# Attention with a top-32 mask: GpSimd's three instructions of a step in another order, and the token step moved up in VectorE's step

## The chip, the cores and the metric

One core of a Trainium2 chip runs the whole program in one launch. The metric is device microseconds (us) of one execution; the figure for a kernel is the median of its runs. Engines are named as in the profile: PE (TensorE), DVE (VectorE), ACT (ScalarE), POOL (GpSimd), SP (the DMA queue).

## What is computed

Three layers follow each other: masked attention, a mixture of experts that sends each token to one expert, and a mixing layer with a Fourier transform and a feed-forward net. The change touches the first alone.

```python
scores = scale * np.matmul(q, k.transpose(0, 1, 3, 2))          # 4 x 8 heads, 576 x 576, head_dim 64
kth = np.partition(scores, -32, axis=-1)[..., -32:-31]          # 32nd largest of each row
scores = np.where(scores >= kth, scores, -1000000000.0)
scores = scores - np.max(scores, axis=-1, keepdims=True)
attn = np.exp(scores)
attn = attn / (np.sum(attn, axis=-1, keepdims=True) + 1e-09)
return np.matmul(attn, v)
```

The gate of the experts is computed from the attention output, token by token, with a carry along the sequence (a token can keep the expert of the token before it).

## The kernel before, in words

**Tiles and steps.** The 4 x 8 heads make 16 pairs, each pair nine tiles of 128 query rows by 576 keys: 144 tiles. The loop over n does, in every step, one operation of each kind for a tile that is some steps behind (table `OFF`). A step of one tile has on each engine:

- PE: the score products `s` (L408), the transposes `tp`/`tr`/`trq` with the mask added (L514, L515), the product with v `u` (L533).
- ACT: the copy of the scores `ss` (L423), `g` (L450: the sign of score against a candidate, with a count beside it), `bb` (L492: the mask), `et` (L521, L522: exponentials), `st_x` (L540, L542: results).
- DVE: eight `MAX8` on pieces of the row (L429, "segments"), five operations on the 64 candidates (L439 to L443), then, for a tile three steps older, `MAX8` over the masked row `y` (L460) and the choice of the threshold `sc` (L466, `select`).
- POOL: `kb` (L471, `lift`: threshold times a constant, one column), and two long passes over 576 columns, `y = ss * g` (L455, `below`) and `z = ss - max` (L501, `shifted`). At a pair's last tile two small copies `ext` (L504) follow `z`.

**Who needs whom.** `sc` needs L460, which needs `y` of the same tile, made two steps earlier. `kb` needs `sc` of the same step; `bb` needs `kb` a step later. `y` needs `g`, made a step earlier. `z` is read by the transposes four steps later. `ss` has six buffers, `z` five, `y` two.

**Order.** Every engine runs its own instructions in the order in which the program issues them. Two strings set it: `ORDER` (L748) is the order of the kinds within a step, where `m` is `z`, `y` is `y` and `dve` the whole of VectorE's part; `DVE_ORDER` (L749) is the order inside that part, which takes the next item of a queue per letter: `s` a segment, `c` a candidate operation, `y` in turn L460, `sc` and `kb` (this one goes to POOL), `t` a token step.

**Token steps.** When a batch of 36 tiles is through (n = 43, 79, 115), the generator `tokens` (L547 on) is queued; each `t` advances it to its next `yield`. Its steps are small DVE operations on tokens and experts (L553 to L644), two POOL products `xtok` in each of its first five steps (L558), PE transposes into the PSUM tiles `tr` and `u`, and five POOL scatters `xs_d` (L656, with a memset L662) at its end. Three batches run their token steps inside the loop; in the third, `ranks` (L223 to L244) follows. The fourth batch runs after the loop.

`tr` is a part of the PSUM tile `trk` that the token steps use too, and every DVE operation that touches it waits for ACT's last use of that tile: `et` (L522) of every second tile, `hi`, `vt` and `in_v` (L323, L368, L379) in the others.

Of the kernel before, what the change touches and what calls it, by code (L numbers as in the profile page):

```python
# [20 lines left out]
B, H, S, D = 4, 8, 576, 64  # L21
# [84 lines left out]
def body(ctx: ExitStack, tc, q, k, v, w_gate, w_local, w1, w2, ch1, ch2, ts, tcd, tnd, tid, out, dbg=None):  # L106
# [149 lines left out]
    def attention(exact):  # L256
# [3 lines left out]
        with ExitStack() as ph:  # L260
# [456 lines left out]
            if exact:  # L717
                for o in zops:
                    o()
                for n in range(n_tile):  # L720
                    i, t = divmod(n, 9)
# [23 lines left out]
            tok, prep, wops = [], [], []  # L745
            OFF = dict(u=8, s=-1, S=-1, t=6, av=7, b=5, m=2, e=6, c=1, y=2, z=4)
            WARM = 64
            ORDER = "t u s m p b e dve y S c av"  # L748
            DVE_ORDER = "ycyscsscsyctscscss"  # L749

            def step_dve(n):
                segs = seg_ops(n) if ok(n) else []
# [9 lines left out]
                queues = dict(c=cnds, s=segs, y=ys, t=[tokstep])  # L762
                for o in DVE_ORDER:
                    if queues[o]:
# [11 lines left out]
            def prep_step(eng):  # L776
                if prep and prep[1] == eng:
                    prep[1] = next(prep[0], "")

            OPS = dict(u=step_u, s=scores, S=evac_s, t=trans, av=av, b=step_b, m=shifted, e=evac_e,  # L780
                       c=count, y=below)
            for n in range(n_tile + 1 + max(OFF.values())):
                i, t = divmod(n, 9)
# [3 lines left out]
                if (n - OFF["t"]) % 2:  # L787
                    prep_step("pe")
                for o in ORDER.split():
                    if o == "dve":  # L790
# [24 lines left out]
            if "kth" in dbg:  # L815
                ACT.dma_start(dbg["kth"], kth)

    attention(False)
    def rows_of(ix, n, em):

# [93 lines left out]
    with tc.If(slow > 0):  # L914
        failed = nc.values_load(fail_i[0:1, 0:1], min_val=0, max_val=1)
        with tc.If(failed > 0):
            attention(True)
        overflow()
# [557 lines left out]
```

## Time and profile before

| | us |
|---|---|
| median of three runs | 1330.04 |
| lowest, highest | 1327.12, 1330.62 |
| profiled execution | 1326.02 |
| span of the profiled execution | 1324.2 |
| attention, loop and drain | about 9 to 557 |
| busy DVE, ACT, POOL over the span | 917.2, 695.9, 535.2 |

The span runs from the first to the last instruction. Busy times of the whole span mix three layers; the change concerns the first 560 us, where the stretches without token steps (9 to 133, 252 to 278, 383 to 410 us: "plain" below) have to be told from those with them. The profile's wait lists name the engine that ended an idle time; where two instructions of different engines overlap and one is longer than usual, no idle time shows, only the longer duration.

### The profile page before, as it was taken

To read this page: it belongs to the slowest core of one execution; us is meant where nothing else is said; L and a number is where in the kernel's file an instruction comes from. 1 tells how busy PE (TensorE), PEld (TensorE's weight loads), DVE (VectorE), ACT (ScalarE), POOL (GpSimd) and SP (SyncE) were. 2 spreads that over 40 slices of the span, in tenths; PEclk is the share of its full clock that TensorE was granted. 3 is DMA by queue.
4 is the path that set the end of the run, shared out by engine and by line. 5 is a ranking of instruction groups with operands and counts; after the bars stand their busy time and mean duration, and the time that the engine had idled before them with its cause. 6 is when DMAs were issued, how large, how long until landed. Compare 5 with 4: busy or idle time off the path is not lost. (4 is left out here: it accounts for less than half of the span.)

```text
span 1324.2 us, 25516 instructions
## 1 busy us (share of the span) xinstructions
PE 1209.5 (91%) x8601; PEld 1090.9 (82%) x8601; DVE 917.2 (69%) x3567; ACT 695.9 (53%) x1752; POOL 535.2 (40%) x693
## 2 busy tenths in 40 slices
PE   6999899898889888299999997888999999999997
PEld 4999788887778777188888886778999999999996
DVE  7999899999999997456566665775763444443222
ACT  6999888898889886144444453232321222221110
POOL 5888777888698877311100011451210000000111
PEclk9999989899999999599999999689999999999999
DMA  4656524343344212386666674654230100100111
GB/s 111 191 141 191 128 68 99 89 109 82 90 102 96 68 28 102 107 292 226 221 210 218 221 238 144 202 159 125 73 128 1 64 32 33 63 2 1 49 48 49
DMA packets 127208, 152.25 MB, mean 115 GB/s; under 512 B 68192, under 2 KB 72536, under 8 KB 126955
## 3 DMA queue, kind: packets, MB, share of 16 engines
q1 hardware_dynamic: 121994, 133.34, 34.7%
q0 software_dynamic: 5072, 17.19, 3.6%
q8 instruction: 69, 1.13, 0.4%
q14 instruction: 73, 0.59, 0.1%
HBM read 92.05 MB, written 32.79 MB: 94 GB/s over the span
## 5 line engine op out<-in xcount | busy, mean ns | idle before, releaser
L429 DVE MAX8 cd<-ss 128x8 f32<-128x72 f32 x1152 | 216.2, 218 | 1.6 <-ACT ss L423 1.4
L1391 DVE SCALAR_TENSOR_TENSOR fhl<-f,fhh 128x256 fp32r<-128x256 f32 x144 | 61.0, 424 | 207.3 <-ACT fhh L1390 207.1
L533 PE MATMUL u<-in_v,et 128*128 128x74 f32 (+1 forms) x1600 | 188.9, 268 | 14.9 <-ACT st_x L540 9.6
L1390 ACT ACTIVATE fhh<-f 128x256 fp32r<-128x256 f32 x144 | 55.1, 383 | 279.2 <-PE f L1386 279.2
L533 PEld LDWEIGHTS u<-in_v,et 128*128 128x128 f32 (+1 forms) x1600 | 179.4, 183 | 24.7 <-ACT st_x L540 16.2
L455 POOL TENSOR_TENSOR y<-ss,g 128x576 f32<-128x576 f32 x144 | 184.9, 1284 | 24.1 <-ACT st_x L540 10.3
L501 POOL TENSOR_TENSOR z<-ss,mt 128x576 f32<-128x576 f32 x144 | 167.1, 1160 | 11.8 <-DVE cd L429 9.6
L1411 POOL DMA_INDIRECT out_dram<-ut,orow x18 | 17.4, 969 | 319.7 <-DVE ut L1407 317.7
L450 ACT ACTIVATE g<-ss,mt 128x576 bf16<-128x576 f32 x144 | 120.0, 834 | 28.9 <-DVE mt L443 26.9
L514 PE MATMUL tp<-ident,z 128*128 128x128 f32 x576 | 120.4, 289 | 15.0 <-DVE lo L326 13.9
L408 PE MATMUL s<-kt,qp 128*128 128x288 f32 x640 | 127.9, 329 | 2.8 <-DVE qp L357 1.6
L492 ACT ACTIVATE bb<-ss,kb 128x576 bf16<-128x576 f32 x144 | 117.9, 819 | 8.7 <-POOL kb L471 8.7
L423 ACT ACTIVATE ss<-s 128x288 f32<-128x288 f32 x288 | 112.5, 472 | 4.4 <-PE s L408 2.7
L460 DVE MAX8 y<-y 128x8 f32<-128x576 f32 x144 | 106.8, 742 | 10.8 <-POOL y L455 10.7
L515 PE MATMUL tp<-neg_id,bb 128*128 128x128 bf16 x576 | 108.8, 223 | 3.8 <-ACT bb L492 3.8
L825 POOL DMA_INDIRECT xm_d<-ysb,sid x23 | 23.6, 1025 | 219.2 <-ACT ysb L1053 215.8
L514 PEld LDWEIGHTS tp<-ident,z 128*128 128x128 f32 x576 | 87.4, 152 | 25.5 <-POOL y L455 6.8
L211 DVE TENSOR_TENSOR wlo<-raw,whi 128x1024 fp32r<-128x1024 f32 x70 | 86.4, 1273 | 23.3 <-ACT whi L210 23.0
L408 PEld LDWEIGHTS s<-kt,qp 128*128 128x128 f32 x640 | 96.8, 202 | 6.1 <-ACT kt L358 3.1
L1386 PEld LDWEIGHTS f<-nxh,whi 128*128 128x128 f32 x576 | 87.7, 188 | 14.1 <-issue 1.2
L521 ACT ACTIVATE et<-tp 128x512 f32<-128x512 f32 x144 | 91.8, 637 | 4.0 <-PE tp L515 4.0
L1402 PE MATMUL f<-whi,fhh 128*128 128x512 f32 x288 | 91.6, 399 | 0.7 <-ACT fhh L1390 0.7
(264 smaller groups left out, 2990.1 us busy)
## 6 DMA issues: line engine op xcount, KB each, us to landing
raw<-in_moe_w_dram SPq DMA_DIRECT2D x32, 1024.0 KB
kt<-hi SPq DMA_DIRECT2D x60, 144.0 KB
kt<-lo SPq DMA_DIRECT2D x60, 144.0 KB
xs_d<-xtok SPq DMA_DIRECT2D x8, 1056.0 KB
fr<-in_moe_w_ch_dram SPq DMA_DIRECT2D x16, 512.0 KB
raw<-in_moe_w_ch_dram SPq DMA_DIRECT2D x16, 512.0 KB
md<-md_d SPq DMA_DIRECT2D x9, 516.0 KB
in_k<-in_k_dram SPq DMA_DIRECT2D x32, 128.0 KB
```

The costliest lines, as they stand in the source:

```text
L408: PE.matmul(p, QP[i][:, s, o:o + 128].bitcast(F32R), KT[i][j][:, s, c].bitcast(F32R), start=(s == heads[0] and j == 0), stop=(s == heads[- ...
L423: ACT.activation(t[:, 288 * hf:288 * hf + 288], SPS.pop((n, hf)), AF.Copy)
L429: return [lambda j=j: DVE.max(cd[:, 8 * j:8 * j + 8], SS[n][:, 72 * j:72 * j + 72]) for j in range(8)]
L450: ACT.activation(g, SS[n], AF.Sign, bias=MT[i][:, t, 1, 7:8], scale=-SCL, accum_out=DIF[n])
L455: POOL.tensor_tensor(y, SS[n], LT[n], op=OP.mult)
L460: DVE.max(y8, Y8[n])
L492: ACT.activation(t, SS[n], AF.Relu, bias=KB.pop(n), scale=-HUGE)
L501: POOL.tensor_tensor(ZZ[n], SS[n], bcast(MT[i][:, t, 0, 0:1], [128, S]), op=OP.subtract)
L514: PE.matmul(o, z[:, k], ident, start=True, stop=False, is_transpose=True)
L515: PE.matmul(o, bb[:, k], neg_id, start=False, stop=True)
L521: ACT.activation(et[:, 0:4], p0.rearrange("p (c n) -> p c n", c=4), AF.Exp)
L533: PE.matmul(p[0:m, s, 0:VW], et[:, kc, qs], vv[:, kc, VC[s]], start=(kc == 0), stop=(kc == 4))
```

## The change

```diff
-            ORDER = "t u s m p b e dve y S c av"
-            DVE_ORDER = "ycyscsscsyctscscss"
+            ORDER = "t u s p b e dve m y S c av"
+            DVE_ORDER = "ycyytscsscscscsscs"
```

On POOL, a plain step early in the loop issued these before the change (one group of three is a step of the cycle; `kb` is the lifted threshold, `y` and `z` the long passes):

```order
L455 TENSOR_TENSOR y<-ss,g 128x576
L501 TENSOR_TENSOR z<-ss,mt 128x576
L471 TENSOR_SCALAR kb<-kth 128x1
L455 TENSOR_TENSOR y<-ss,g 128x576
L501 TENSOR_TENSOR z<-ss,mt 128x576
```

and these with it:

```order
L471 TENSOR_SCALAR kb<-kth 128x1
L501 TENSOR_TENSOR z<-ss,mt 128x576
L455 TENSOR_TENSOR y<-ss,g 128x576
L471 TENSOR_SCALAR kb<-kth 128x1
L501 TENSOR_TENSOR z<-ss,mt 128x576
```

So `y` no longer stands right behind `kb`; `z` of the same tile stands between, where it used to be issued ahead of `kb`. The products `xtok` and the scatters of a token step stay behind `kb`, now with `z` and `y` behind them.

On DVE, the step of the first batch that holds the token operation L589 read, from the choice `sc` on, before the change

```order
L466 SCALAR_TENSOR_TENSOR sc_3877,kth<-iotan,dif,y_3874 128x8
L429 MAX cd<-ss 128x8
L440 MATCH_REPLACE cw<-mt,cd 128x64
L429 MAX cd<-ss 128x8 x2
L441 MAX m8b<-cw 128x8
L429 MAX cd<-ss 128x8
L442 MATCH_REPLACE cw<-m8b,cw 128x64
L589 TENSOR_TENSOR dl<-fr,iom_118 128x40
L429 MAX cd<-ss 128x8
L443 MAX mt<-cw 128x8
```

and with it

```order
L466 SCALAR_TENSOR_TENSOR sc_3875,kth<-iotan,dif,y_3872 128x8
L589 TENSOR_TENSOR dl<-fr,iom_118 128x40
L429 MAX cd<-ss 128x8
L440 MATCH_REPLACE cw<-mt,cd 128x64
L429 MAX cd<-ss 128x8 x2
L441 MAX m8b<-cw 128x8
L429 MAX cd<-ss 128x8
L442 MATCH_REPLACE cw<-m8b,cw 128x64
L429 MAX cd<-ss 128x8
L443 MAX mt<-cw 128x8
```

The token operation moved ahead of four segments and three candidate operations; the rest keeps its order. PE, ACT and SP issue what they issued, in the same order.

## Rows read from the trace of the kernel before

**Rows 1.** Busy us by stretch: one plain, one token-heavy of each kind.
```profile
core 0: us, PE busy (x) PEld busy (x) DVE busy (x) ACT busy (x) POOL busy (x), PEclk, DMA share, GB/s
...
50.50:133.10 82.60, 81.70 (x766) 77.18 (x767) 82.60 (x499) 81.97 (x241) 71.20 (x88) 1.00 0.64 174
...
171.00:229.00 58.00, 55.28 (x457) 50.81 (x456) 54.38 (x303) 47.94 (x134) 42.32 (x51) 0.88 0.35 82
229.00:252.30 23.30, 19.83 (x144) 17.86 (x145) 22.20 (x111) 17.31 (x48) 20.10 (x28) 0.78 0.45 120
```
**Rows 2.** Groups by line, DVE then POOL, 50.5 to 133.1 us: busy, mean ns | idle before.
```profile
L466 DVE SCALAR_TENSOR_TENSOR sc<-iotan,dif,y 128x8 f32<-128x8 f32 x27 | 12.2, 450 | 0.0
```
```profile
L455 POOL TENSOR_TENSOR y<-ss,g 128x576 f32<-128x576 f32 x27 | 34.7, 1287 | 5.4 <-ACT st_x L540 3.2 <-ACT g L450 0.6
```
**Rows 3.** Timeline of POOL near 91 us: start, duration, last the idle time before.
```profile
91.56 1.29 POOL L455 TENSOR_TENSOR y<-ss,g 128x576 f32<-128x576 f32 x1 [0.79 <-ACT st_x L540]
```
**Rows 4.** Groups by line and form, DVE, 143 to 515 us.
```profile
L611 DVE TENSOR_TENSOR_SCAN po<-ones,slot,er 8x576 f32<-8x576 f32 x3 | 5.7, 1889 | 0.0
...
L627 DVE TENSOR_TENSOR pr<-pr,oh 128x40 f32<-128x40 f32 x3 | 3.0, 994 | 0.0
...
L620 DVE SCALAR_TENSOR_TENSOR cnt<-pcol,po 8x1 f32<-8x1 f32 x3 | 1.9, 627 | 0.0
...
L242 DVE TENSOR_TENSOR rcb<-capr,roh 8x8 f32<-8x8 f32 x1 | 0.9, 867 | 0.0
...
L225 DVE SCALAR_TENSOR_TENSOR rkey<-first,rkey 8x1 f32<-8x1 f32 x1 | 0.7, 690 | 0.0
```
**Rows 5.** The same view, 534 to 541 us: the fourth batch, after the loop.
```profile
L611 DVE TENSOR_TENSOR_SCAN po<-ones,slot,er 8x576 f32<-8x576 f32 x1 | 1.4, 1406 | 0.0
...
L627 DVE TENSOR_TENSOR pr<-pr,oh 128x40 f32<-128x40 f32 x1 | 0.2, 193 | 0.0
...
L620 DVE SCALAR_TENSOR_TENSOR cnt<-pcol,po 8x1 f32<-8x1 f32 x1 | 0.1, 136 | 0.0
```
**Rows 6.** Timeline near 188 us: a token operation and the POOL pass beside it.
```profile
188.00 1.28 POOL L455 TENSOR_TENSOR y<-ss,g 128x576 f32<-128x576 f32 x1
...
188.61 0.74 DVE L589 TENSOR_TENSOR dl<-fr,iom 128x40 f32<-128x40 f32 x1
```
**Rows 7.** Timeline of DVE: end of `sc`, and the segment after the second MATCH_REPLACE.
```profile
62.97 0.08 DVE L466 DVE_READ_ACCUMULATOR sc<-iotan,dif,y 128x1 f32 x1
...
64.03 0.22 DVE L429 MAX8 cd<-ss 128x8 f32<-128x72 f32 x1
```
**Rows 8.** Waits of DVE, 20 to 515 us: us in total, times, longest.
```profile
DVE oe L626 <- ACT et L522: 4.2, 3, 1.5
DVE dl L581 <- ACT pr L579: 1.9, 1, 1.9
...
DVE exi L240 <- ACT et L522: 0.8, 1, 0.8
DVE rgt L233 <- ACT et L522: 0.5, 1, 0.5
DVE oh L623 <- ACT in_v L379: 0.4, 2, 0.2
```
**Rows 9.** Waits of POOL, 143 to 515 us.
```profile
POOL kb L471 <- DVE sc L466: 37.8, 44, 1.8
...
POOL xtok L558 <- DVE ri L554: 2.9, 2, 1.5
```
**Rows 10.** Timeline near 231 us: `sc` in the stretch of the scatters.
```profile
231.53 1.85 DVE L466 SCALAR_TENSOR_TENSOR sc<-iotan,dif,y 128x8 f32<-128x8 f32 x1
...
232.20 1.15 POOL L501 TENSOR_TENSOR z<-ss,mt 128x576 f32<-128x576 f32 x1
```
**Rows 11.** Timeline of POOL: the first token step of the first batch.
```profile
148.24 1.19 POOL L558 TENSOR_TENSOR xtok<-st_x,ri 128x256 f32<-128x256 f32 x2 [4.86 <-DVE cd L429]
149.39 1.28 POOL L455 TENSOR_TENSOR y<-ss,g 128x576 f32<-128x576 f32 x1
```

## The prediction

> **What bounds the kernel now.** I read the busy times by stretch first. In a plain stretch (the first of [rows 1]) ACT is busy 81.97 of 82.60 us and DVE all of it, POOL 71.20. These two numbers do not weigh the same. DVE's is partly standing: its choice `sc` takes 450 ns on average [rows 2], while its input is eight columns. ACT's is work. So ACT sets the pace of plain steps, and what DVE or POOL wait for there is spare. In the token stretch (the second of [rows 1]) it is the other way round: DVE 54.38 of 58.00, ACT 47.94, POOL 42.32; there DVE sets the pace, and POOL mostly waits for it: 37.8 us before `kb` in 44 waits between 143 and 515 us [rows 9].
>
> Then I read what DVE does in that stretch, by line. Nine kinds of small token operation run between 627 and 994 ns there (L627 the longest, L620 the shortest [rows 4]; L581, L583, L589, L591, L599 and both copies of L636 between them), 6.82 us for one of each. In the fourth batch, which runs with no long POOL pass beside it, such operations take 136 to 193 ns [rows 5], about 1.60 us for all nine (for five of them, which other POOL work holds there too, I take the price of an operation of like form). The timeline shows why: L589 starts at 188.61, when POOL's `y` is under way since 188.00, and lasts until 189.35, just past the end of `y` at 189.28 [rows 6]. A token operation that DVE issues inside a POOL pass stands until that pass ends. The position before the change is what puts it there: DVE gets to the token step 1.06 us after `sc` [rows 7], while `kb` and then `y` start right after `sc`.
>
> **The change, part by part.** No work is added or removed.
>
> *Token steps right behind `sc`.* POOL's `kb` waits for `sc`, so in a step where DVE is late POOL is idle when the token operation is issued; it runs at its free price. Nine kinds: (6.82 - 1.60) x 3 batches = 15.7 us. The scan L611: 1889 - 1406 ns [rows 4, 5], x 3 = 1.4. The five held operations of `ranks` (690 to 867 ns [rows 4], 3.66 together, against 0.87 free in the fourth batch): 2.8. Together 19.9 us, the upper bound. Not all of it is reached: L627 and L242 stand behind an operation that still waits for ACT (next term), so that POOL is in its passes again; I count half of their 0.80 x 3 + 0.72, and 0.2 x 3 for the second copy L636, which meets `kb`. That leaves **17.7 us gained**, all on DVE where it sets the pace.
>
> *Waits that this exposes.* A token operation that needs ACT or PE is now reached 1.06 us earlier [rows 7], and the seven operations that used to run meanwhile stand behind it, with `y`'s L460 and the next `sc` after them. Operations that already wait today wait longer by all of it: L626 three times, L581 once, L240, L233, L623 twice [rows 8], eight in all: 8.5 us. Of L604, L606, L613 and the third L623, which wait little or not at all today, I count one half of 1.06 for the last. **9.0 us lost.** The bounds: nothing, if the producers come earlier by as much, and 20 such operations x 1.06 = 21.2 if every one of them is exposed (six a batch, two in `ranks`).
>
> *`z` ahead of `y`.* In plain steps it covers `y`'s wait for `g`: 5.4 us in 82.6 [rows 2], of which 0.79 in one step [rows 3]. Over the plain stretches, some 177 us, that is 11.6 as the upper bound; but ACT, which makes `g`, has only 0.63 us spare per 82.6 [rows 1], 1.4 over them. I take **1.4 gained**, by the row it is nearest to, since ACT's work stays the same.
>
> In the first five token steps of a batch POOL also has `xtok` and is late: DVE waits for `y` there. The first `y` after the stall (`xtok` at 148.24, `y` at 149.39 [rows 11]) now has a `z` of 1.15 [rows 10] ahead of it: 3 x 1.15 = 3.5 lost, a delay that is not made up, since POOL stays the slower one until DVE takes over. Two of the three stalls are waits for DVE's `ri` (2.9 together [rows 9]), which the earlier token step shortens by 1.06 each: 2.1 back. The last tile's `y` in the drain comes behind its `z` as well: 1.15. Together **2.5 lost**.
>
> *The scatter stretch* (229 to 252 us, and the like in the second batch): POOL is busy 20.1 of 23.3 [rows 1] and `sc` waits through both passes (1.85 us from 231.53 to 233.38 [rows 10]). POOL's cycle holds the same instructions in either order; I count nothing. If POOL's cover there went, the cost would be DVE's, which has slack.
>
> Here the Trainium skill has a rule, in "SBUF — State Buffer", section "SBUF: two separate sides": a GpSimd instruction and a VectorE one with two SBUF inputs (or in a two-port mode) hold a shared port pair for their whole length, whoever starts first, and the other stands. The row on L589 agrees. By the rule the loser changes sides: `kb` would stand behind the token operation. The rows on `sc` do not follow it alone: by it `sc` would have got in at the end of `y` at 232.25, and it stood through `z` too.
>
> Sum: -17.7 + 9.0 - 1.4 + 2.5 = **-7.6 us**. The profiled execution took 1326.0 us, 4.0 below the median; the difference goes onto the median: 1330.0 - 7.6 = **1322.4**.
>
> **The rivals.**
>
> *The port changes sides.* A token operation started ahead of `kb` holds POOL: 1.41 for each scan, 0.2 for the 32 others, 10.6 us, if all of it reached the end: 1330.0 + 3.0 = 1333. Against it: POOL waits 0.86 us on average before `kb` there (37.8 / 44 [rows 9]), which covers the small ones, and a scan's step is long on DVE. With half of it the time is 1328, no change. The skill's rule above gives the same mechanism.
>
> *More than the forecast.* The waits are not absolute: ACT and PE, whose own work waits for DVE's token operations, come earlier too. With 2 us of waits instead of 9 the gain is 14.6 and the time 1315. For it: PE and ACT have spare time in the token stretch [rows 1]. Against: ACT follows DVE through `g` and is then nearer to its limit.
>
> *Slower.* Every token operation that touches `tr` or `u` stands right behind `sc` for ACT's use of it, the whole 1.06, and holds all segments of its step: 21.2 instead of 9.0, so +4.6; with `sc` held through `xtok` and both passes in the first steps of a batch, as it is in the scatter stretch [rows 10], one more pass of 1.15 a batch, +8: 1338. It decides from 16 of the 20 operations on ((17.7 + 1.4 - 2.5) / 1.06). For it: ACT in plain steps runs late against DVE, and after a gain it would be so in token steps.
>
> That the change does nothing is ruled out by the order of the instructions, which moved as described.
>
> **How the numbers follow.** About 0.3% (4 us) is what a measurement of this kernel can tell from no change. Forecast (1318 to 1326) 0.42; more 0.18; port or ACT takes the gain back (1326 to 1334) 0.24; slower 0.16. Nearly all of the forecast's own range is a gain of over 4 us, so faster 0.58, same 0.26, slower 0.16. The range goes from the 17.7 reached with hardly any new wait (1311) to the edge of the slower case (1335).
>
> **What would show it.** In the profile after: the nine kinds at 0.14 to 0.25 us in the loop; idle time of DVE before L626, L623, L581, L233, L240 up by about 1 us each and little before L604, L606, L613; POOL's `y` without idle time for `g`; plain stretches as long as before with ACT still busy; `sc` ending with `y` where it ended with `z`. The prediction is wrong if token operations stay at 0.7 us (held by `kb` or `z`), if DVE's new waits exceed 17 us, or if plain steps change by more than 1%.

## The result and the profile after

The changed kernel takes **1348.31 us** (median of 4 runs, 1337.02 to 1350.13) against 1330.28 before (4 runs): ratio 1.0132, 95% interval 1.0096 to 1.0168, 18 us slower. The forecast was 1322.4, the range 1311 to 1335: wrong in sign, and outside the range. The ratios below leave out runs more than 1.5% above the fastest of their kernel; for e6 and e13 this drops all runs above 1332 us, and the text gives those.

The profiled execution (1348.31 us) is 22.3 us longer than that of before. All of it lies in the attention loop: from the end of `sc` of tile 0 to that of tile 143 it takes 520 us against 497.4. I call the time from the end of tile k's `sc` to the end of the next "step k", and add the steps up by kind (worked out from the ends of L466 in the timelines; the last three columns are experiments below):

```
steps                                            before  after     e2     e7     e8
17 with L581, L604, L606, L623, L626, L233, L240   64.6  102.0   79.2   81.9   68.2
34 other token steps                              123.8  106.5  109.0  106.5  109.0
21 with xtok (39-45, 75-81, 111-117)               80.9   83.3   79.9   83.7   80.2
14 with scatters (61-67, 97-103)                   54.0   53.3   56.3   53.0   55.4
57 others                                         174.2  175.0  178.2  174.6  177.2
```

Two things happened at once: 34 token steps became 17.3 us shorter, as forecast, and 17 became 37.4 us longer. (In 14 of the 17 an operation waits; in the three with L606 it is L607 that is held, 2.7 us of the 37.4.) Busy time by stretch, after (the first two stretches answer to [rows 1]; the others are one step that waits, with its neighbours):

```profile
core 0: us, PE busy (x) PEld busy (x) DVE busy (x) ACT busy (x) POOL busy (x), PEclk, DMA share, GB/s
50.50:133.10 82.60, 82.08 (x768) 77.14 (x767) 79.59 (x500) 82.20 (x242) 71.30 (x89) 1.00 0.66 177
171.00:229.00 58.00, 53.89 (x416) 49.87 (x417) 44.11 (x272) 42.90 (x121) 37.10 (x45) 0.82 0.28 65
304.00:308.00 4.00, 2.82 (x24) 2.39 (x22) 4.00 (x27) 2.77 (x9) 3.84 (x5) 1.00 0.03 7
308.00:312.00 4.00, 2.50 (x14) 2.22 (x15) 3.96 (x22) 3.03 (x9) 3.64 (x6) 0.55 0.45 106
312.00:316.00 4.00, 4.00 (x21) 4.00 (x20) 1.90 (x12) 1.80 (x5) 3.62 (x5) 0.50 0.50 113
316.00:320.00 4.00, 4.00 (x24) 3.41 (x24) 1.20 (x11) 2.68 (x8) 0.65 (x1) 0.50 0.00 0
320.00:324.00 4.00, 4.00 (x36) 3.75 (x34) 4.00 (x26) 2.90 (x7) 2.20 (x3) 0.74 0.33 76
```

The plain stretch is as before. In the token stretch DVE, ACT and POOL are all less busy (DVE 44.11, was 54.38): none of the three is the bound there. PE's granted clock is 0.82 (was 0.88), and around 312 us it is 0.50, the lower of its two levels (1.2 GHz); in the three slices from 312 to 324 us PE is the one engine that is busy throughout.

The operations themselves, by line, 143 to 540 us; they answer to [rows 4], and all but L607 run at or near free prices [rows 5]:

```profile
L611 DVE TENSOR_TENSOR_SCAN po<-ones,slot,er 8x576 f32<-8x576 f32 x3 | 4.2, 1401 | 0.0
...
L607 DVE TENSOR_TENSOR pr<-pr,psm 128x40 f32<-128x40 f32 x3 | 3.4, 1123 | 0.0
...
L627 DVE TENSOR_TENSOR pr<-pr,oh 128x40 f32<-128x40 f32 x3 | 0.6, 193 | 0.0
...
L589 DVE TENSOR_TENSOR dl<-fr,iom 128x40 f32<-128x40 f32 x3 | 0.6, 189 | 0.0
...
L620 DVE SCALAR_TENSOR_TENSOR cnt<-pcol,po 8x1 f32<-8x1 f32 x3 | 0.4, 138 | 0.0
L242 DVE TENSOR_TENSOR rcb<-capr,roh 8x8 f32<-8x8 f32 x1 | 0.2, 217 | 0.0
```

And DVE's waits, 20 to 540 us (us in total, times, longest); they answer to [rows 8]:

```profile
DVE dl L581 <- ACT pr L579: 14.1, 3, 4.9
DVE oe L626 <- ACT et L522: 11.7, 3, 4.1
DVE oh L623 <- ACT in_v L379: 10.8, 3, 3.8
DVE er L604 <- ACT vt L368: 7.2, 3, 2.5
...
DVE ri L553 <- ACT st_x L542: 2.1, 3, 1.0
DVE rgt L233 <- ACT et L522: 1.5, 1, 1.5
DVE exi L240 <- ACT et L522: 1.2, 1, 1.2
```

That is 48.6 us, where [rows 8] add up to 7.8. One of them, the wait of L581 in step 83, in the timeline after:

```profile
309.50 0.45 PE L514 MATMUL tp<-ident,z 128*128 128x128 f32 x1 [1.90 <-DVE lo L326]
...
313.81 0.08 DVE L466 DVE_READ_ACCUMULATOR sc<-iotan,dif,y 128x1 f32 x1
313.99 0.21 POOL L471 TENSOR_SCALAR kb<-kth 128x1 f32<-128x1 f32 x1 [0.30 <-DVE sc L466]
...
314.24 2.25 PE L375 MATMUL tr<-wg,vt 128*128 128x18 f32 x10
...
316.52 0.31 ACT L379 ACTIVATE in_v<-tr 128x45 f32<-128x45 f32 x2 [1.81 <-PE tr L375]
...
316.71 0.78 ACT L492 ACTIVATE bb<-ss,kb 128x576 bf16<-128x576 f32 x1
...
318.37 0.27 ACT L522 ACTIVATE et<-trq 128x128 f32<-128x128 f32 x1
318.52 0.24 ACT L579 ACTIVATE pr<-dl 128x40 f32<-128x40 f32 x1
318.80 0.18 DVE L581 TENSOR_SCALAR dl<-dl 128x40 f32<-128x40 f32 x1 [4.90 <-ACT pr L579]
```

and the same places in the kernel before:

```profile
305.03 1.23 PE L375 MATMUL tr<-wg,vt 128*128 128x18 f32 x10
...
307.10 1.09 DVE L466 SCALAR_TENSOR_TENSOR sc<-iotan,dif,y 128x8 f32<-128x8 f32 x1
...
308.12 0.08 DVE L466 DVE_READ_ACCUMULATOR sc<-iotan,dif,y 128x1 f32 x1
...
308.24 0.29 ACT L522 ACTIVATE et<-trq 128x128 f32<-128x128 f32 x1
...
308.39 0.26 ACT L579 ACTIVATE pr<-dl 128x40 f32<-128x40 f32 x1
...
309.18 0.72 DVE L581 TENSOR_SCALAR dl<-dl 128x40 f32<-128x40 f32 x1
```

`pr` stands in ACT's queue behind `st_x`, `in_v`, `bb` and `et` of the step. Before, `sc` itself took 1.09 us (after, 0.22), so ACT was through with them 0.45 us after the end of `sc`, and L581 came later still: no wait. After, `sc` is early, ACT ends `pr` 4.9 us behind it, and DVE stands with all segments and candidates of the step behind it; `g`, `y` and the next `sc` wait for those. The ten matmuls of L375 take 2.25 us in place of 1.23: PE is at half clock, after it stood 1.90 us for DVE's L326.

### The profile page after: what moved, and what is told of

Read it like the earlier page. It is cut to its first block, busy times and chain, and to the rows that moved or that the text cites. A ratio compares the mean times of both kernels' runs of the same rounds, so it can differ in the third digit from the quotient of the medians.

```text
span 1346.5 us, 25516 instructions
## 1 busy us (share of the span) xinstructions
PE 1231.0 (91%) x8601; PEld 1111.0 (83%) x8601; DVE 894.7 (66%) x3567; ACT 698.6 (52%) x1752; POOL 537.1 (40%) x693
## 5 line engine op out<-in xcount | busy, mean ns | idle before, releaser
L533 PE MATMUL u<-in_v,et 128*128 128x74 f32 (+1 forms) x1600 | 201.1, 280 | 12.5 <-ACT st_x L540 8.9
L533 PEld LDWEIGHTS u<-in_v,et 128*128 128x128 f32 (+1 forms) x1600 | 191.7, 194 | 22.3 <-ACT st_x L540 16.2
L514 PE MATMUL tp<-ident,z 128*128 128x128 f32 x576 | 123.7, 294 | 16.3 <-DVE lo L326 14.1
L408 PE MATMUL s<-kt,qp 128*128 128x288 f32 x640 | 132.0, 336 | 3.7 <-DVE qp L357 1.6
L515 PE MATMUL tp<-neg_id,bb 128*128 128x128 bf16 x576 | 112.0, 227 | 4.4 <-ACT bb L492 4.4
L408 PEld LDWEIGHTS s<-kt,qp 128*128 128x128 f32 x640 | 100.2, 208 | 7.3 <-ACT kt L358 3.1
```

What stands on the lines that cost most here:

```text
L408: PE.matmul(p, QP[i][:, s, o:o + 128].bitcast(F32R), KT[i][j][:, s, c].bitcast(F32R), start=(s == heads[0] and j == 0), stop=(s == heads[- ...
L514: PE.matmul(o, z[:, k], ident, start=True, stop=False, is_transpose=True)
L515: PE.matmul(o, bb[:, k], neg_id, start=False, stop=True)
L533: PE.matmul(p[0:m, s, 0:VW], et[:, kc, qs], vv[:, kc, VC[s]], start=(kc == 0), stop=(kc == 4))
```

## The experiments

**Theory W:** a token operation right behind `sc` waits for ACT's and PE's work of the same step, DVE's candidates stand behind it, and that is the loss. **Rival P:** POOL's order (`z` behind `kb`) is the loss. **Rival C:** the loss is PE's halved clock. **Rival F:** the freed operations are worth nothing. All medians, with the ratio to the kernel before in the same session (its medians were 1326.7 to 1328.3):

```
e1  POOL's order alone                     1330.70 (12 runs)  1.0027 [1.0010, 1.0043]
e2  token step's place alone               1333.82 (10)       1.0051 [1.0032, 1.0069]
e3  token step last in DVE's step          1336.82 (6)        1.0076 [1.0054, 1.0099]
e4  waiting token steps last               1324.19 (12)       0.9985 [0.9969, 1.0002]
e5  old POOL order, waiting ones late      1328.10 (12)       1.0009 [0.9994, 1.0024]
e6  changed kernel, both cures of waits    1316.08 (13)       0.9905 [0.9892, 0.9918] (7 runs)
e7  changed kernel, extra matmuls          1331.15 (12)       1.0032 [1.0009, 1.0054]
e8  as e6, old POOL order                  1319.36 (7)        0.9950 [0.9930, 0.9969]
e9  e6 with the extra matmuls              1329.63 (12)       1.0005 [0.9986, 1.0024]
e10 mixed version, extra matmuls           1322.19 (11)       0.9948 [0.9931, 0.9965]
e11 kernel before, extra matmuls           1331.43 (12)       1.0024 [1.0006, 1.0042]
e12 kernel before, both cures of waits     1324.13 (12)       0.9976 [0.9958, 0.9993]
e13 e9 with half the matmuls               1338.59 (12)       0.9951 [0.9920, 0.9982] (the lower runs)
e14 e10 with half the matmuls              1318.24 (12)       0.9941 [0.9916, 0.9965]
e15 changed kernel, pr early alone         1341.93 (6)        1.0128 [1.0090, 1.0166]
e16 changed kernel, pt moved alone         1337.19 (6)        1.0070 [1.0045, 1.0094]
e17 e14, memset early                      1320.16 (12)       0.9951 [0.9929, 0.9973]
e18 e17 without extra matmuls              1317.57 (12)       0.9940 [0.9915, 0.9965]
```

**The two halves (e1, e2).** Each is one string of the change:

```diff
-ORDER = "t u s m p b e dve y S c av"
+ORDER = "t u s p b e dve m y S c av"
```
```diff
-DVE_ORDER = "ycyscsscsyctscscss"
+DVE_ORDER = "ycyytscsscscscsscs"
```

> POOL's half of the change alone: lift first, then z and y; the token step keeps its old place, about 1.06 us behind sc. Theory W (the 18 us come from token operations that now stand right behind sc and wait there for ACT's work of the same step, 47 us of DVE waits against 8 before): the waits go back to about 8 us, the two long passes hold the operations about as before, so the time is 1322 to 1336 us, that of the kernel before within 0.5%. Theory P (the moved z makes the transposes late, and that is the loss): 1343 to 1353 us, that of the changed kernel.

> The other half alone: the token step right behind sc, POOL's order as before (z ahead of the lift). Theory W: L581, L604, L623 and L626 wait 2 to 5 us each time, 35 to 50 us in all, and the time is 1338 to 1356 us. Theory P: 1320 to 1334 us, since z is where it was.

e1 is where W has it (with 13.4 us of these waits, not 8), and rival P falls with it: POOL's order costs 0.3%. e2 lies below W's range, at the upper edge of P's: it is slower, but its waits are 23.7 us (L623 6.9, L626 5.6, L581 4.1, L604 3.5, the rest 3.6), not 35 to 50. But 0.27% and 0.51% do not add up to 1.32%: the halves make each other worse. Most of the difference goes with the clock. In e2 it is 1.00, 1.00 and 0.94 in the three token stretches (the first below), in the changed kernel 0.82, 0.82 and 0.85; the 17 steps take 79.2 us in e2, 102.0 in the changed kernel, and 81.9 when its clock is held up (e7).

```profile
171.00:229.00 58.00, 51.18 (x464) 46.27 (x464) 52.65 (x313) 48.73 (x141) 44.53 (x55) 1.00 0.35 82
```

The order has a part in it as well: in a plain step `et` ends 2.7 us behind `sc` with the new POOL order (2.2 with the old one, shown below), so the same place behind `sc` is earlier against ACT.

**The token step elsewhere (e3, e4, e5).** In e3 `t` is last:

```diff
-DVE_ORDER = "ycyytscsscscscsscs"
+DVE_ORDER = "ycyyscsscscscsscst"
```

In e4 a new letter `T` takes the steps whose `yield` in `tokens` or `ranks` says that they wait (`yield 1`), and `t` only the others, one step in all per n:

```diff
-DVE_ORDER = "ycyytscsscscscsscs"
+DVE_ORDER = "ycyytscsscscscsscsT"
...
-                yield
+                yield 1
                 oh = ap.tile([128, 5, 8], F32, name="oh", bufs=1)
```

e5 has `T` at the old place, the old `ORDER`, and `pr` issued a step ahead of L581:

```diff
+DVE_ORDER = "ycyytscsscscTscsscs"
```

> The changed kernel with the token step moved to the end of DVE's step, behind the last segment and candidate. Theory W: what is left of a wait stands behind the candidates and delays no g, so 1314 to 1332 us; waits of L581, L604, L623, L626 each 1.5 us shorter at least. Theory P: still 1340 to 1352 us, as POOL's order is the changed one.

> The changed kernel, but the steps that wait for ACT or PE (ri, L581, L604, L623, L626, L233, L240) go to the end of DVE's step; the others stay right behind sc. Theory W: the free operations keep their 0.14 to 0.20 us, the waits before L581, L604, L623 and L626 fall from 47 us to under 15, and the time is 1308 to 1322 us, below both kernels. Theory P: 1340 to 1352 us.

> POOL's order of the kernel before; token steps right behind sc, but those that wait (ri, L604, L623, L626, L233, L240) stand where the token step stood before, and pr is issued a step ahead of L581, so L581 waits for nothing. Theory W (the waits are the loss): about 6 us of waits are left (L626 1.4 us three times, L233, L240), some 14 of 20 token operations a batch run at 0.2 us, and the time is 8 to 16 us below the kernel before, 1311 to 1319 us. Rival F (the operations freed from POOL's passes are worth little, since ACT sets the step): within 4 us of the kernel before.

e3 misses W's range (1314 to 1332). It has only 8.2 us of waits and is still 0.8% slower than before: at the end of the step the operations meet POOL's passes again, and longer (by line and form, 143 to 520 us; at most 0.2 us in the changed kernel):

```profile
L583 DVE TENSOR_TENSOR dl<-dl,iota 128x40 f32<-128x40 f32 x3 | 3.5, 1176 | 0.0
...
L589 DVE TENSOR_TENSOR dl<-fr,iom 128x40 f32<-128x40 f32 x3 | 3.3, 1099 | 0.0
```

So being held is a price of its own, and W alone does not explain e3. e4 gets the whole loss back (from 1.0132 to 0.9985), but misses its range: L581 still waits 7.3 us in three. e5 misses by 9 us: in the steps of L623 and L626 (57 and 58: 6.0 and 6.4 us against 3.1 and 5.2 before) the clock is halved, and they wait 8.1 and 7.5 us in all. Its time is where rival F has it, within 4 us of the kernel before; e8 and e12 below decide on F.

**The waits taken away at their source (e6, e8, e12, e15, e16).** `pr` (ACT's reading of `dl`) moves one step ahead of L581, which overwrites `dl`; `pt` and the ranks move out of the PSUM tile that the transposes use:

```diff
                 DVE.memset(tk[0:1, 0, :], 2.0)
-                yield
                 pr = ap.tile([128, 5, 8], F32, name="pr", bufs=1)
                 ACT.activation(pr, dl, AF.Exp)
+                yield
                 DVE.tensor_scalar(dl, dl, 0.0, -8.0, op0=OP.is_ge, op1=OP.mult)
...
-            rank_ps[0] = tkp
+            tkq = ub[:, 352:512]
+            rank_ps[0] = tkq
...
-                pt = tkp[:, 0:80].rearrange("p (t e) -> p t e", t=5)
+                pt = tkq[:, 0:80].rearrange("p (t e) -> p t e", t=5)
```

e6 is the changed kernel with both, e8 the same with the old `ORDER`, e12 with both old strings; e15 and e16 are the changed kernel with the first or the second alone.

> The changed kernel in both orders, but what the token operations wait for is taken away: pr is issued a step ahead, and the ranks and the turned positions (pt) stand in columns 352 to 511 of u's PSUM tile, not beside the transposes of z. Theory W: L581, L623, L626, L233 and L240 wait under 0.5 us each, L604 (2.1 to 2.5 us, three times) and ri (2 us in all) stay, so waits fall from 47 to some 10 us and the time to 1308 to 1322 us. Rival P (POOL's order) or rival C (the halved TensorE clock by itself, with the waits hidden): above 1336 us.

> As the run without the shared bank, but with POOL's order of before (z ahead of the lift, y behind). Theory W, by which POOL's order matters only in the steps with the first token operations (39 to 46, 75 to 82 and 111 to 118 took 1.4, 1.6 and 0.8 us longer in the changed kernel): 2 to 6 us below the run without the shared bank. Rival P: far below it, by 10 us or more; if the lift behind z costs: above it.

> POOL's order and the token step's place as before the change, but pr a step ahead and the ranks and pt in u's tile: the wait cure without either half of the change. Theory: the waits were only 8 us here and the operations stay held by POOL's passes, so 1318 to 1327 us; the distance to the run with the same cure, the old POOL order and the token step right behind sc (1319.4) is what the place is worth once it costs no waits, 0 to 8 us. Rival F (the place is worth nothing): the same time as that run within 2 us.

> The changed kernel with pr issued one step ahead of L581 and nothing else. L581's waits (4.3, 4.9 and 4.9 us) go: 1330 to 1338 us if a wait costs what the trace shows before it; 1342 to 1350 us if another wait or the halved clock takes its place in the next steps.

> The changed kernel with pt and the ranks in u's tile and nothing else. The waits of L623 and L626 (3.4 to 4.1 us, six of them) and L233, L240 shrink to those of the run without the shared bank (0.7 and 1.4 us), 17 us less: 1325 to 1335 us; together with pr early that makes the 1316 to 1339 us of the run with both.

With the two orders untouched and the waits cut from 48.6 to 18.2 us (in its profile, of a run of 1339.5), e6 turns the loss into a gain in seven of its 13 runs, which lie at 1313 to 1316 us. The other six lie at 1333 to 1344, with a mean granted clock of 0.937 to 0.947 against 0.961 to 0.965; the mean of all 13 is 1325.6, no better than before. e8 holds 1317 to 1324. e12 against e8 (0.9976 and 0.9950, 3.5 us) is what the place is worth with both cures, though e8 still has 14.7 us of waits and e12 5.3: a fifth of the 17.7 forecast. The two intervals overlap, so that it is more than rival F's nothing is likely, and not settled. By steps, against the kernel before, e8 has 14.8 us in the 34 free steps and gives 8.0 back, in the waiting steps (3.6), the scatter steps (1.4) and the others (3.0).

e16 brings 8 us (17 expected) and misses its range: the waits of L626 are now for `u`'s reader and short, L581's stay. Waits of DVE, 20 to 530 us (one line was added, so the numbers are one higher):

```profile
DVE dl L582 <- ACT pr L580: 11.8, 3, 4.9
...
DVE oe L627 <- ACT st_x L541: 4.0, 3, 1.4
```

That the wait moved from `et` to `st_x` shows it was for the reader of the same PSUM tile, not for data. The Trainium skill has a reason, in "PSUM — Partial Sum Buffer", section "PSUM bank collisions raise a hardware error": two engines may not touch one bank and 32-partition quadrant at the same time, reads included, and it is for the software to keep such accesses apart. The wait of L627 (4.0 us) agrees; no run shows the error.

e15 lands at the edge of its second case (1342 to 1350): 14 us of waits gone and nothing gained. Steps 83 to 85 together fall only from 13.3 to 11.9 us: L581 does not wait, and steps 84 and 85 run at half clock (4.5 and 4.7 us for 2.8).

**The clock held up (e7, e9, e11, e13).** Eight matmuls whose results are unused fill PE's stand for L326 in six steps (e13: the three ahead of L581):

```diff
+                if n in (50, 60, 86, 96, 122, 132):
+                    for _ in range(8):
+                        PE.matmul(trq, ident, ident, start=True, stop=True)
                 for o in ORDER.split():
```

> The changed kernel with eight matmuls more ahead of the transposes in six steps (two a batch) where TensorE stood 1.4 to 1.9 us for VectorE just before its granted clock fell from 1.0 to 0.5; their results are used by nothing. Theory W: if the clock stays at 1.0, the waits before L581 and L623 shrink by the slower matmuls' part, from 4.9 and 3.5 us to about 2.5, some 10 us in all, and the time to 1330 to 1340 us; most of the loss stays. Rival C (the clock is the loss, the waits follow from it): 1330 us or below, with waits under 20 us. If the clock falls all the same: 1343 to 1352 us.

> The run without the shared bank with the eight extra matmuls of the warm run in the same six steps. Theory: two losses add up, the waits (15 us at full clock) and the halved clock that TensorE falls into where it stands for VectorE (13 us). With both away: granted clock 0.958 or more, every run within 1308 to 1320 us, none of the 1333 to 1344 us that 6 of the 13 runs without the extra matmuls took. If those runs had another cause than the clock, they come back here.

> The kernel before with the eight extra matmuls in the same six steps. Theory: its clock fell in one of three batches only (0.88, 0.97 and 1.00 in the stretches of the three), so they bring 0 to 4 us: 1322 to 1328 us. If the matmuls are a gain by themselves, whatever the token step does: 1310 to 1318 us.

> No shared bank, both new orders, extra matmuls only in the three steps ahead of L581. If the two groups of the run without them are the clock: all runs in one group, 1310 to 1322 us, clock at least 0.958, and steps 48 and 49 at 2.8 us where the 1339.5 us run had 5.3 and 4.9. If not the clock: some runs above 1330 us again.

In e7 the clock stays at 0.98 to 1.00 in the token stretches, and L581 waits 1.7 us where it waited 4.9. Windows, then waits (20 to 530 us):

```profile
171.00:229.00 58.00, 53.62 (x488) 48.81 (x488) 52.13 (x306) 47.69 (x138) 42.15 (x51) 1.00 0.35 81
304.00:359.00 55.00, 50.64 (x460) 45.88 (x459) 49.14 (x293) 44.84 (x129) 39.17 (x47) 1.00 0.33 77
433.00:512.00 79.00, 73.49 (x669) 67.65 (x667) 70.09 (x436) 66.06 (x188) 59.19 (x72) 0.98 0.20 51
```
```profile
DVE dl L581 <- ACT pr L579: 5.1, 3, 1.7
DVE oe L626 <- ACT et L522: 4.4, 3, 1.5
DVE oh L623 <- ACT in_v L379: 4.3, 3, 1.4
DVE er L604 <- ACT vt L368: 3.6, 3, 1.2
```

All waits come to 22.6 us, and the kernel from 1.0132 to 1.0032. W's range holds that time, but not W's claim that most of the loss stays: 13 of the 18 us are the clock's, and perhaps more, since the extra matmuls may cost something too. Rival C is right on that much, and no more: e7, at full clock, still pays 17.3 us in the 17 waiting steps, all that the other token steps gain. e11 misses its range (1322 to 1328): on the kernel before the matmuls won nothing, and the clock went from 0.88, 0.97 and 1.00 in the three token stretches to 0.97, 1.00 and 0.94.

e9 is a miss: one group of runs, as expected, at 0.954 to 0.961, but at 1325 to 1334, not 1308 to 1320. The second place costs (step 57 takes 5.5 us against 3.5 in e6, some 6 us in three batches); the rest stays open, as no profile of e6's lower group was taken. With the first place alone (e13) the two groups are back: four runs at 1314 to 1324, one at 1331, seven at 1338 to 1346. By the words of its expectation that speaks against the clock, but its profile (1343.9 us) shows the clock falling elsewhere. Steps 48 and 49 are at 2.8 us, and the clock falls ten steps later instead, around step 93:

```profile
349.00:353.00 4.00, 4.00 (x27) 3.85 (x26) 1.95 (x18) 0.29 (x1) 2.75 (x4) 0.50 0.50 112
353.00:357.00 4.00, 4.00 (x22) 3.69 (x22) 1.09 (x6) 2.27 (x7) 1.35 (x2) 0.50 0.23 52
```

There L626 waits 4.9 us (1.4 in e6). So in this run the cure of one place left the fall to a later one, where PE stands again (1.61 us, for L613).

**Mixed versions (e10, e14, e17, e18).** The old `ORDER`, the token step right behind `sc`, both cures of e6, and L604's step alone at the old place (`T` as in e5); e10 with six steps of extra matmuls, e14 with three; e17 is e14 with `pt` cleared eight steps earlier, e18 the same without extra matmuls:

```diff
-                pt = tkq[:, 0:80].rearrange("p (t e) -> p t e", t=5)
-                DVE.memset(pt, 0.0)
...
                 DVE.tensor_reduce(mx, lg[:, :, 0:8], axis=AX.X, op=OP.max)
+                pt = tkq[:, 0:80].rearrange("p (t e) -> p t e", t=5)
+                DVE.memset(pt, 0.0)
```

> Token step right behind sc, POOL's order of before, pr a step ahead, pt and the ranks in u's tile, the step of L604 alone at its old place, and the extra matmuls. By the sum: the run with the old POOL order and no shared bank (1319.4) less L604's 4.4 us of waits less a few us of clock: 1308 to 1317 us, the fastest here.

> The mixed version (old POOL order, token step right behind sc, L604's step at its old place, no shared bank) with the extra matmuls in three steps rather than six. The second place cost about 2.8 us a batch (steps 56 and 57: 3.59 and 4.78 us against 2.79 and 2.80 without): 1310 to 1318 us, 4 to 9 us below the run with six.

> As the mixed version with extra matmuls in three steps, but pt is cleared eight steps earlier, in the step of L569, so that u's matmuls in step 56 do not stand for the memset behind L611's scan. If that stand is what the clock falls after: step 58 takes 5.2 us or less in place of 8.1, step 57 2.8 in place of 4.9, every run lies within 1306 to 1320 us, at a clock of 0.96 or more. If the clock falls all the same: 1313 to 1331 us as without.

> The same without any extra matmul. If the stand ahead of step 47 (1.9 us behind VectorE's L326) is enough for the clock to fall: some runs at 1325 to 1340 us with half-clock steps at 47 to 49, clock 0.95 or less; if with the old POOL order it is not: 1306 to 1318 us, the fastest here.

All four beat both kernels, the one before by 0.5 to 0.6%; their intervals overlap, and no order among them is shown. e10 misses its range (the second place again), e14 touches its upper end. e17 lands in its second case: a stand of 1.4 us for L326 is left ahead of step 57, and the clock falls behind it in all three batches (step 58 and its likes take 7.7 to 8.0 us); with the same stand e18 shows it in the third alone (5.2, 5.1 and 7.7 us in steps 58, 94 and 130). The simplest, e18, is the version to keep.

## Why the prediction was wrong, point by point

- **Token steps right behind `sc`, 17.7 gained: right.** The 34 token steps that wait for nothing are 17.3 us shorter, the operations at 0.14 to 0.22 us. That the two numbers meet is in part luck: 2.6 of the 17.3 are in steps 46, 82 and 118, whose operations were free before too, and some 3 of the 17.7 are for L581, L627 and L242, which stand in waiting steps. Like for like it is 14.7 forecast and 14.7 measured. One not foreseen: L607, second in its step behind the scan L606, now meets `z` and takes 1123 ns (231 before).
- **Waits that this exposes, 9.0 lost: this step failed.** Measured: 40.8 us more of waits (the prediction itself took more than 17 as a sign of being wrong) and 37.4 us on the 17 steps. e7, at full clock, keeps 17.3 of the 37.4; the other 20.1 come with the halved clock. It went wrong three ways.
  - *The clock.* The prediction has no term for it, and L581 stands 4.9 us where e7 shows 1.7.
  - *The count.* e7 has 14.8 us more of waits than the kernel before, and 12.9 of them are with L581, L623, L604 and `ri`, of which the prediction counts three waits and a half. They waited little before because DVE came to them late (to L581 in step 83 behind an `sc` of 1.09 us, and all of them by the 1.06 us of the old place); now 17 operations wait (three each of L581, L604, L623, L626 and `ri`, and L233 and L240), not "eight in all".
  - *The size.* The words "wait longer by all of it" took the distance moved, 1.06 us, as the price. L626, counted three times at that price, waits no longer in e7 (1.5 at most, as before) and up to 4.1 in the changed kernel. The price is the time from `sc` to the end of the producer in the same step. A figure for it stood in the trace, in any plain step of the kernel before:

```profile
87.58 0.08 DVE L466 DVE_READ_ACCUMULATOR sc<-iotan,dif,y 128x1 f32 x1
...
89.58 0.29 ACT L522 ACTIVATE et<-trq 128x128 f32<-128x128 f32 x1
```

  `et` ends 2.2 us behind `sc` there: more than the longest waits of e7 (1.0 to 1.8 us), less than those of L581, L604, L623 and L626 in the changed kernel (2.5 to 4.9).
- **`z` ahead of `y`, 1.4 gained in plain steps: no.** The 57 other steps are 0.8 us longer; the plain stretch takes the same time, with ACT as the bound, as argued. **2.5 lost at `xtok` and in the drain:** these 21 steps are 2.4 us longer, but the agreement is luck. Only 1.4 of the 2.5 was for them; the 1.15 for the drain does not show, since outside the loop the execution became no longer. By halves, e1 loses 3.2 us in these steps (3.5 forecast) and e2 gains 0.9 (2.1 forecast).
- **The scatter stretch, nothing:** 0.7 us shorter.
- **The rivals.** The slower case had the mechanism, its place and its sign, but with the whole 1.06 as the highest price of a wait; twelve waits at 2.1 to 4.9 us were outside what it could give. The port changed sides for the scan alone: with L611 started ahead of it `kb` takes 1.24 us, in all three batches, where 0.21 is usual, and that step is still 0.5 us shorter than before. Beside the small operations `kb` starts 0.09 us behind `sc` and takes 0.21, as before. "Nearly all of the forecast's own range is a gain" rested on the 9.0.

```profile
207.41 1.40 DVE L611 TENSOR_TENSOR_SCAN po<-ones,slot,er 8x576 f32<-8x576 f32 x1
207.57 1.24 POOL L471 TENSOR_SCALAR kb<-kth 128x1 f32<-128x1 f32 x1 [1.55 <-DVE sc L466]
```

- **The sum with the measured terms:** -17.3 + 37.4 + 2.4 - 0.7 + 0.8 = 22.6, the profiled execution's 22.3 within 0.3. With e7's steps the loop is 2.4 us longer than before, the extra matmuls included: at full clock the 17 steps alone take back what the freed operations give.

## What to carry to other kernels

When an instruction that waits is moved up on an in-order engine, price the wait by where its producer ends in the same step, read on the producer's engine, and not by the distance moved: an instruction that has not waited may have been saved by the very delay that the change removes. Then ask what the standing engine starves: here the candidates behind it, and with them the work of the next step on POOL, ACT and PE; and look at PE's granted clock in the profile after, since here it made more than half of the loss. Take away the wait first (read a step earlier, another PSUM tile), and move the work after that.

## What the runs showed of the hardware

TensorE's mean granted clock goes with the time of a run as much as the order does: the same kernel e6 took 1313 to 1316 us at 0.961 to 0.965 and 1333 to 1344 at 0.937 to 0.947, and the changed kernel 1348 to 1350 at 0.939 to 0.941 and 1337 at 0.953. Ahead of the falls in the token steps that I looked at PE had stood 1.4 to 1.9 us for VectorE. But a stand of 1.77 us in the kernel before was followed by a fall in one batch of three, and one of 1.76 in e2 by none, so a stand does not settle it; what does stays open. The Trainium skill, "TensorE: Matmul & The Clock Gate", section "What's actually happening", says that the low level is the default and activity releases it, and that the watch runs free of the kernel's start; the runs, in which the fall comes and goes in one kernel, fit that, and do not show the cause. At half clock PE's work is late and DVE waits longer (L581 4.9 us, at full clock 1.7); whether the waits in turn keep the clock down is not shown.

VectorE and GpSimd hold each other up both ways: small DVE operations issued into a POOL pass stood until its end ([rows 6], and longer in e3), and POOL's one-column `kb` stood 1.24 us beside DVE's scan L611, started 0.16 us earlier.
